# Two tiles transposed by the DMA engines instead of TensorE, and six units computed in halves of 256 columns

## The chip, the cores and the metric

The kernel runs on one core of a Trainium2 chip. Five engines work on it side by side, each with an instruction queue that is executed in order: TensorE (PE; its weight loads are shown apart as PEld), VectorE (DVE), ScalarE (ACT), GpSimd (POOL) and SyncE (SP). They wait for one another through semaphores. Transfers are done by 16 DMA engines; a transfer is issued by a queue, here SP's (q1 in the profile) or ScalarE's (q10). TensorE writes into PSUM, eight banks of 128 x 512 fp32 values. The metric is the device time of one execution in microseconds.

## The reference

`x` is 2048 tokens of 512 values in bf16. The output is `x` plus a linear attention with learnt softmax features plus a dense layer pair with Mish, both fed by the same layer norm:

```python
xn = _layernorm(x, axis=-1)                       # no scale, no shift, eps 1e-5
return x + _A_ref(xn, A_wqkv, A_w_phi, A_wo) + _B_ref(xn, B_w1, B_b1, B_w2)
# _A_ref: H = 32 heads of Dh = 16
pq = jnp.einsum("bhsd,hdf->bhsf", q, w_phi)       # the same for k
phi_q = jnp.concatenate([_softmax(pq, axis=-1), _softmax(-pq, axis=-1)], axis=-1)
kv = jnp.einsum("bhsf,bhsd->bhfd", phi_k, v)
z  = jnp.einsum("bhsf->bhf", phi_k)
num = jnp.einsum("bhqf,bhfd->bhqd", phi_q, kv)
den = jnp.einsum("bhqf,bhf->bhq", phi_q, z)[..., None] + 1e-6
o = num / den                                     # heads joined, then @ wo
# _B_ref: F = 1792
h = jnp.einsum("bsd,df->bsf", x, w1) + b1
act = h * jnp.tanh(sp)                            # sp = softplus(h)
return jnp.einsum("bsf,fd->bsd", act, w2)
```

## The kernel before

**Tiles and groups.** The tokens are 16 tiles of 128, in 4 groups of 4. `xnT` holds the normalised tokens transposed: for each tile four blocks of 128 channels by 128 tokens. It is needed by every projection: as the stationary operand for logits and values, as the moving operand for the first dense layer.

**The order by hand.** `STEPS` is one list of steps, executed from left to right when the program is built (lines 623 to 625). Every step appends its instructions to the queues of its engines. So the list fixes, for each engine, the order of its own work; between engines only data and buffers are waited for. `@n` names one of six PSUM banks (a shared buffer: a new owner waits until the old contents have been read); `a` and `v` say whether ScalarE or VectorE does the copy or inversion.

**The steps that matter here.**

- Opening, first group, tile by tile: `LS i` (statistics of tile i, VectorE), `RS i` (the inverse root, GpSimd), `AZ i` (normalise, VectorE), `TP i` (four TensorE transposes of 128 columns into a bank, line 560), `TC i` (copy into `xnT`, line 565).
- `F0 kt` (fold: key weights times the feature weights, four matmuls of 128 columns, line 156), `FD kt` (copy to `wkp`, line 165); `F`, `FC` the same for the queries. `WB` builds the block matrix for the folds, `KM` a mask, `PB` and `CB` turn and copy the bias.
- `LP`: the logits of tiles 0 and 1, eight matmuls of 512 columns (line 209), in pairs: both tiles with fold 0, then both with fold 1, and so on.
- `V t` (values of tile t, line 194) and `VC t` (copy, line 218); `L s i` (logits of stage s, tile i) and `LC s i` (copy, line 252); stages 0 to 3 are the keys of the groups, 4 to 7 the queries. `WL` is a logit step in the two banks beside the six.
- `H u` (unit u of the first dense layer: 128 of the 1792 hidden channels for one group of 512 tokens, four matmuls of 512 columns, line 228); u = 0 to 13 is group 0, 14 to 27 group 1. `M u` (Mish on ScalarE, line 239) frees its bank.
- `LN g`, `AP g k`: statistics of group g, and normalisation of its half k with a DMA transpose of two tiles issued by SP (line 186). `DX g` loads the tokens of group g (SP), `DW` loads the second layer's weights `w2` (2, three DMAs) and `wo` (3), `WT` the query weights.
- Softmax: `E s 0/1` (maxima and minima, VectorE, five operations each), `X` (exponentials, ScalarE), `S` (sums, VectorE), `R` (inversion), `N` (normalise), `A` (key-value matrices, TensorE); `KV`, `W`, `Q`, `G`, `C` for the queries; `C h` ends in a DMA transpose issued by SP.
- `O t` (second dense layer for tile t, 14 matmuls), `P t` (output projection), `Y t` (residual, and the store); `OH`, `PH`, `YH` the last tile in two parts.

ScalarE keeps one table set at a time: `M` needs one, `X`, `R a`, `W a` and `C a` another; the program loads a table when the set changes (line 138).

Before `STEPS` the loads are issued: on SP tile 0, the key weights transposed (`wT`), tiles 2 and 3, `wv`, half of `w1`, tiles 4 to 7, the other half of `w1`; on ScalarE the feature weights, tile 1 and the bias (lines 483 to 493). Twelve matmuls on constants run first (line 513).

Of the kernel before, what the change touches and what calls it, by code (L numbers as in the profile page):

```python
# [29 lines left out]
9; M 10; AP 1 1; H 11 @5; E 0 1; V 4 @1; X 0 1; WL 1; LN 2; V 6 @4; VC 4 a; X 0 0; L 1 0 @2; L 1 3  # L30
@0; LC 1 0 a; V 5 @3; LN 3; VC 5 a; H 12 @1; WL 2; H 13 @2; VC 6 a; S 0 0; LC 1 3 a; M 11; V 3 @3; M
12; M 13; H 14 @4; H 15 @0; H 16 @5; H 17 @1; VC 3 a; M 14; H 18 @2; M 15; M 16; M 17; LC 1 2 a; H
19 @3; AP 2 0; AP 2 1; AP 3 0; L 2 0 @4; LC 2 0 a; L 2 1 @0; LC 2 1 a; V 2 @5; S 0 1; L 2 2 @1; M
18; LC 1 1 a; M 19; H 20 @4; LC 2 2 a; AP 3 1; H 21 @0; WT; H 22 @2; M 20; VC 2 a; R 0 1 v; L 2 3
@3; H 23 @1; R 0 0 v; N 0 1; M 21; N 0 0; H 24 @4; M 22; LC 2 3 a; F 0 @5; F 1 @0; E 1 0; E 1 1; M
23; M 24; F 2 @2; E 2 0; E 2 1; FC 0 a; H 25 @3; H 26 @1; FC 1 a; H 27 @4; M 25; M 26; L 3 2 @5; FC
2 a; M 27; V 7 @0; L 3 3 @3; V 11 @1; F 3 @2; L 3 0 @4; LC 3 0 v; LC 3 2 a; L 3 1 @5; A 0 0; X 1 0;
X 1 1; A 0 1; LC 3 3 a; FC 3 v; S 1 0; V 8 @4; LC 3 1 a; VC 7 a; L 4 0 @2; E 3 0; VC 8 a; LC 4 0 a;
L 4 1 @3; LC 4 1 a; L 4 3 @5; VC 11 a; L 4 2 @0; X 2 0; V 9 @4; L 5 0 @2; H 28 @3; H 29 @1; VC 9 a;
LC 4 2 v; M 28; M 29; H 30 @0; H 31 @4; H 32 @3; M 30; H 33 @1; H 34 @0; M 31; M 32; M 33; M 34; H  # L40
35 @4; M 35; H 36 @3; M 36; S 1 1; LC 4 3 a; R 1 0 v; E 3 1; LC 5 0 a; N 1 0; R 1 1 v; H 37 @1; H 38
@0; H 39 @4; H 40 @3; H 41 @5; H 42 @2; S 2 0; A 1 0; M 37; N 1 1; M 38; M 39; M 40; A 1 1; M 41; M
42; X 3 0; L 6 3 @1; L 5 2 @0; V 10 @4; VC 10 a; L 5 1 @3; LC 5 2 a; L 6 0 @5; E 4 0; E 4 1; X 2 1;
S 3 0; V 15 @2; VC 15 a; V 13 @4; VC 13 a; LC 6 0 a; R 2 0 a; S 2 1; DW 3; R 3 0 a; X 3 1; L 6 1 @0;
LC 5 1 a; DW 2; N 3 0; N 2 0; L 5 3 @2; O 0 @4; S 3 1; V 12 @5; V 14 @3; LC 6 1 a; LC 5 3 a; O 1 @0;
L 6 2 @2; R 2 1 a; N 2 1; VC 14 a; LC 6 3 a; VC 12 v; R 3 1 a; N 3 1; X 4 0; A 2 0; S 4 0; LC 6 2 a;
A 2 1; A 3 0; W 4 0 v; X 4 1; H 43 @3; M 43; A 3 1; H 44 @1; H 45 @5; M 44; H 46 @2; M 45; H 47 @3;
M 46; M 47; H 48 @1; KV; H 49 @5; H 50 @2; Q 0 0; M 48; M 49; G 0 0; M 50; H 51 @3; H 52 @1; H 53
# [2 lines left out]
S 5 0; Q 1 0; L 7 3 @5; G 1 0; E 6 1; W 5 0 a; P 0; P 1; Y 0; Q 1 1; O 4 @1; G 1 1; LC 7 3 a; O 5
@4; S 5 1; Q 2 0; O 6 @5; C 1 a; P 2; G 2 0; W 5 1 v; Y 1; Q 2 1; P 3; O 7 @0; E 7 0; X 6 0; S 6 0;
G 2 1; Q 3 0; C 2 a; G 3 0; Y 2; Y 3; X 6 1; O 8 @2; Q 3 1; W 6 0 v; E 7 1; S 6 1; P 4; P 5; G 3 1;
C 3 a; Q 4 0; X 7 0; Y 4; W 6 1 v; X 7 1; S 7 0; O 9 @3; O 10 @1; G 4 0; Q 4 1; P 6; P 7; G 4 1; Y
# [601 lines left out]
```

## Time and profile before

| | us |
|---|---|
| three runs | 173.78, 173.98, 173.88; median 173.88 |
| the profiled execution | 174.0 |
| its span in the profile | 172.3 |
| TensorE busy | 168.7 (98%) |
| VectorE busy | 143.2 (83%) |
| ScalarE busy | 119.5 (69%) |

The span is what the profile covers, from the first to the last instruction; 1.7 us of the execution lie around it. Times in the text are microseconds from the span's start. A timeline line gives the start, the length, the engine, the line of the program, the operation, what it writes and reads, how many instructions it joins, and in brackets the idle time before them with what ended it. In a line on a stretch each engine has its busy time and, in parentheses, its instructions. A matmul's length contains its latency; the distance from one start to the next is what it costs in a row of them.

### The profile page before, as it was taken

The numbers are of one execution on the slowest core, as the hardware profiler recorded it, in microseconds if no ns is written. First come the engines' busy times: TensorE is split into PE (matmuls) and PEld (weight loads), VectorE is DVE, ScalarE is ACT, GpSimd is POOL, SyncE is SP. The second block draws the span as 40 slices with busy tenths as digits, with TensorE's granted clock in tenths as the row PEclk, the third lists the DMA queues.
The fourth block names the chain that finished last, engine by engine and source line by source line (L and its number), as shares of the span: only waits on it lengthen the run. The fifth ranks groups of instructions, "written<-read, shape, count | busy, mean of one in ns | idle before, by whom it ended". The sixth has DMA issues, their size and how long they took to land.

```text
span 172.3 us, 2713 instructions
## 1 busy us (share of the span) xinstructions
PE 168.7 (98%) x1039; PEld 82.4 (48%) x1039; DVE 143.2 (83%) x221; ACT 119.5 (69%) x192; POOL 9.4 (5%) x26
## 2 busy tenths in 40 slices
...
GB/s 98 269 377 365 82 98 0 37 189 207 366 120 0 0 4 0 0 0 0 4 0 0 64 118 66 12 51 67 150 152 93 150 95 144 172 168 100 173 134 61
DMA packets 44953, 18.02 MB, mean 105 GB/s; under 512 B 37004, under 2 KB 44940, under 8 KB 44940
## 3 DMA queue, kind: packets, MB, share of 16 engines
...
q10 hardware_dynamic: 844, 0.25, 0.6%
q8 instruction: 8, 0.13, 0.3%
...
## 4 chain that ended last, share of the span: by engine, by line
PE 95%; DMA 3%; SPq 0%; DVE 0%; issue 0%
PE po L463 28%; PE ph L228 28%; PE pl L194 14%; PE po L470 8%; PE pv L194 8%; DMA wT<-in_A_wqkv_dram 3%; PE pnd L418 2%; PE pkv L387 2%; PE pfold L156 1%; PE pwide L194 1%; PE pl L209 1%; PE ptr L560 0%; SPq L483 0%; DVE x_sb L477 0%; PE pb L533 0%
## 5 line engine op out<-in xcount | busy, mean ns | idle before, releaser
L463 PE MATMUL po<-w_sb,acts 128*128 128x512 bf16 (+2 forms) x238 | 50.7, 366 | 0.0
L228 PE MATMUL ph<-xnT,w_sb 128*128 128x512 bf16 x224 | 50.1, 379 | 0.0
L239 ACT ACTIVATE acts<-ph,b1f 128x512 bf16<-128x512 f32 x56 | 37.2, 694 | 4.6 <-PE ph L228 4.4
L305 DVE TENSOR_REDUCE s<-e 128x128 f32<-128x2048 bf16 x16 | 36.4, 2279 | 2.5 <-ACT e L288 2.5
L228 PEld LDWEIGHTS <-w_sb 128*128 128x128 bf16 x224 | 21.7, 98 | 25.5
L463 PEld LDWEIGHTS <-acts 128*128 128x128 bf16 x238 | 22.3, 98 | 24.1
L288 ACT ACTIVATE e<-e 128x2048 bf16<-128x2048 bf16 x16 | 30.3, 1908 | 0.0
L194 PEld LDWEIGHTS <-xnT 128*128 128x128 bf16 x184 | 17.6, 98 | 20.1 <-DMA wv<-in_A_wqkv_dram 0.2
L252 ACT CAST p_sb<-pl 128x512 bf16<-128x512 f32 x27 | 15.4, 587 | 5.5 <-PE pl L194 4.7
L433 ACT COPY ds<-pnd 128x32 f32<-128x32 f32 x16 | 2.9, 183 | 23.5 <-PE pnd L418 23.5
L194 PE MATMUL pv<-wv,xnT 128*128 128x512 bf16 x64 | 16.1, 379 | 0.0
L477 DVE TENSOR_TENSOR x_sb<-po,x_sb 128x512 bf16<-128x512 f32 (+2 forms) x17 | 10.9, 654 | 5.7 <-PE po L470 5.7
L470 PE MATMUL po<-wqk,xnT 128*128 128x512 bf16 (+2 forms) x68 | 15.5, 366 | 0.0
L194 PE MATMUL pl<-wqk,xnT 128*128 128x512 bf16 x64 | 15.3, 379 | 0.0
L170 DVE BATCH_NORM_STATS2 stats<-x_sb 128x6 f32<-128x512 bf16 x16 | 10.1, 679 | 4.3 <-DMA x_sb<-in_A_x_dram 4.3
L263 DVE TENSOR_TENSOR m<-m 128x512 bf16<-128x512 bf16 (+1 forms) x32 | 11.5, 358 | 1.1
L194 PE MATMUL pl<-wkp,xnT 128*128 128x512 bf16 x48 | 11.7, 379 | 0.0
L263 DVE TENSOR_TENSOR m<-p_sb 128x1024 bf16<-128x1024 bf16 x16 | 10.9, 682 | 0.2 <-ACT p_sb L252 0.2
L272 DVE TENSOR_TENSOR e<-p_sb,m 128x2048 bf16<-128x2048 bf16 x8 | 9.8, 1226 | 1.4 <-PE pkv L387 1.1
L272 DVE TENSOR_TENSOR e<-m,p_sb 128x2048 bf16<-128x2048 bf16 x8 | 9.8, 1225 | 0.3
L340 DVE TENSOR_TENSOR e<-e,r 128x2048 bf16<-128x2048 bf16 x8 | 9.6, 1215 | 0.0
L138 ACT ACT_TABLE_LOAD x7 | 9.0, 1283 | 0.1
...
## 6 DMA issues: line engine op xcount, KB each, us to landing
...
w_sb<-in_B_w_dram SPq DMA_DIRECT2D x2, 896.0 KB, 7.8
x_sb<-in_A_x_dram SPq DMA_DIRECT2D x3, 512.0 KB, 10.0
...
wv<-in_A_wqkv_dram SPq DMA_DIRECT2D x1, 512.0 KB, 4.5
wqk<-in_A_wo_dram SPq DMA_DIRECT2D x1, 512.0 KB, 4.6
w_sb<-in_B_w_dram SPq DMA_DIRECT2D x1, 512.0 KB, 9.6
...
```

What stands on the lines that cost most here:

```text
L170: nc.vector.bn_stats(stats[:, i, :], xs[:, i, :])
L194: nc.tensor.matmul(pp, lhsT=xnT[:, t, kt, :], rhs=w[:, kt, :], start=(kt == 0), stop=(kt == KT - 1),)
L228: nc.tensor.matmul(ph_of[u][:], lhsT=w1_sb[:, kt, f * P : (f + 1) * P], rhs=xnT[:, g * TPG : (g + 1) * TPG, kt, :], start=(kt == 0), stop= ...
L239: nc.scalar.activation(acts[:, f, g * 512 : (g + 1) * 512], ph_of.pop(u)[:], ACT.Mish, bias=b1f[:, f : f + 1])
L252: copy(p_of[s][:, i, :], pl_of.pop((s, i)))
L263: nc.vector.tensor_tensor(out=m[:], in0=src[:, :, 0:half], in1=src[:, :, half : 2 * half], op=op)
L272: nc.vector.tensor_tensor(out=e_of[s][:].rearrange("p t j l c -> p (t j) l c")[:, :, pl, :].rearrange("p t (c e o) -> p t c e o", e=8, o=2 ...
L288: nc.scalar.activation(v, v, ACT.Exp)
L305: nc.vector.reduce_sum(t[:], pair(s, k).rearrange("p t j l (c e) -> p (t j l c) e", e=16), axis=AX.X)
L463: nc.tensor.matmul(po_of[t, c.stop][:, c], lhsT=acts[:, f, t * P : (t + 1) * P], rhs=w2_sb[:, f, c], start=(f == 0), stop=False,)
L470: nc.tensor.matmul(po_of[t, c.stop][:, c], lhsT=oT_of[t // 2][:, t % 2 * 4 + j, :], rhs=wo_sb[:, j, c], start=False, stop=(j == 3),)
L477: nc.vector.tensor_tensor(out=y, in0=po_of.pop((t, c.stop))[:, c], in1=y, op=ALU.add)
```

## The change

- `TP 2`, `TP 3`, `TC 2` and `TC 3` go. In their place stand `AD 2` and `AD 3`: a DMA transpose of one tile each from the normalised tokens straight into `xnT`, issued from ScalarE's queue.
- The units 0 to 5 of the first dense layer are computed in two halves of 256 columns: `HA u b` for tiles 0 and 1, `HB u` for tiles 2 and 3, into the same bank; all six `HA` come first.
- Buffers: sums 6 instead of 3, the logarithm in place of its operand, `r2` 3 instead of 2, `r` 1 instead of 2.
- The order is written anew throughout: among others `TP 1` stands ahead of the folds, all four `FD` are ScalarE's, `DW 2` comes in the opening and `DX 3` later, `LN 2` ahead of `AP 1 0`, and other copies and inversions are ScalarE's or VectorE's than before.

```diff
--- before.py
+++ after.py
@@ -22,40 +22,40 @@
 WARM = 12
 STEPS = """
-LS 0; RS 0; DX 2; LS 1; WB; RS 1; AZ 0; TP 0 @0; F0 0 @1; F0 1 @2; AZ 1; FD 0 v; TP 1 @3; TC 1 v; LS
-2; PB @4; RS 2; TC 0 a; LS 3; RS 3; FD 1 a; AZ 2; F0 2 @5; F0 3 @0; FD 2 a; FD 3 a; LP i @1,2; KM;
-DX 3; AZ 3; V 0 @3; LC 0 0 a; TP 2 @5; V 1 @0; TC 2 a; TP 3 @1; VC 0 a; LC 0 1 v; TC 3 v; CB; L 0 2
-@5; L 0 3 @2; LC 0 3 a; LN 1; H 0 @3; H 1 @1; H 2 @4; M 0; LC 0 2 a; H 3 @2; M 1; M 2; M 3; VC 1 a;
...
-@5; S 4 1; W 4 1 v; M 51; M 52; H 54 @2; H 55 @3; Q 0 1; M 53; E 5 0; E 5 1; M 54; E 6 0; L 7 0 @1;
-M 55; G 0 1; C 0 a; X 5 0; LC 7 0 a; L 7 1 @5; X 5 1; O 2 @2; O 3 @3; LC 7 1 a; L 7 2 @1; LC 7 2 a;
...
-0; O 13 @0; Q 6 1; G 6 1; W 7 1 v; P 8; P 9; Q 7 0; C 6 a; G 7 0; P 10; P 11; Y 8; Q 7 1; G 7 1; O
-14 @2; Y 9; Y 10; C 7 a; P 12; P 13; OH 0 @3; PH 0; Y 11; P 14; OH 1 @1; PH 1; Y 12; Y 13; YH 0; Y
-14; YH 1
+KM; LS 0; LS 1; RS 0; WB; AZ 0; TP 0 @0; TC 0 a; DX 2; RS 1; AZ 1; TP 1 @1; F0 0 @2; F0 1 @3; TC 1
+v; FD 0 a; LS 2; FD 1 a; F0 2 @4; FD 2 a; LS 3; F0 3 @5; RS 2; AZ 2; FD 3 a; AD 2; RS 3; AZ 3; PB
+@0; AD 3; DW 2; LP i @1,2; V 1 @3; V 0 @4; VC 0 a; LC 0 0 v; LC 0 1 a; VC 1 v; HA 0 @5; HA 1 @1; HA
+2 @3; CB; HA 3 @0; HA 4 @4; HA 5 @2; LN 1; HB 0; HB 1; HB 2; M 0; LN 2; AP 1 0; HB 3; L 0 2 @5; HB
+4; M 1; M 2; M 3; M 4; HB 5; H 6 @1; M 5; M 6; L 0 3 @3; LC 0 3 a; AP 1 1; LC 0 2 a; H 7 @0; H 8 @4;
+M 7; H 9 @2; H 10 @1; M 8; DX 3; H 11 @3; M 9; M 10; H 12 @5; E 0 0; M 11; M 12; AP 2 0; H 13 @0; H
+14 @4; M 13; M 14; AP 2 1; WL 1; E 0 1; X 0 0; L 1 0 @2; V 3 @1; LN 3; VC 3 a; LC 1 0 a; L 2 1 @3; L
+2 0 @5; S 0 0; L 2 2 @0; AP 3 0; L 2 3 @4; H 15 @1; H 16 @2; LC 2 0 a; LC 2 1 a; H 17 @5; LC 2 2 a;
+X 0 1; R 0 0 a; M 15; M 16; AP 3 1; WT; WL 2; LC 2 3 v; M 17; H 18 @3; H 19 @0; M 18; LC 1 1 v; E 2
+0; M 19; E 2 1; L 1 3 @4; H 20 @1; H 21 @2; H 22 @5; LC 1 2 a; M 20; LC 1 3 a; M 21; M 22; H 23 @3;
+V 6 @0; E 1 0; S 0 1; M 23; H 24 @1; M 24; H 25 @4; M 25; VC 6 a; H 26 @2; F 0 @5; M 26; F 1 @3; FC
+1 a; H 27 @1; H 28 @4; M 27; H 29 @0; H 30 @2; M 28; M 29; H 31 @3; E 1 1; M 30; M 31; H 32 @1; M
+32; F 2 @4; X 1 0; V 2 @0; V 8 @2; V 4 @3; FC 2 a; FC 0 v; V 9 @5; L 3 1 @1; VC 4 a; R 0 1 v; VC 2
+v; F 3 @0; FC 3 a; N 0 0; A 0 0; VC 8 a; X 1 1; L 3 0 @4; N 0 1; VC 9 v; L 3 2 @3; S 1 0; S 1 1; L 4
+3 @0; L 3 3 @2; LC 3 0 a; LC 3 3 a; LC 3 1 a; L 4 0 @5; V 7 @4; LC 3 2 a; R 1 0 a; R 1 1 a; LC 4 0
+a; X 2 1; VC 7 v; L 4 1 @2; LC 4 1 v; LC 4 3 v; V 5 @1; VC 5 a; L 4 2 @3; V 12 @4; N 1 0; X 2 0; H
+33 @2; A 0 1; H 34 @5; H 35 @0; LC 4 2 v; N 1 1; M 33; M 34; E 3 0; H 36 @3; A 1 0; H 37 @1; A 1 1;
+S 2 1; M 35; E 4 0; H 38 @2; VC 12 a; V 11 @5; M 36; H 39 @0; H 40 @4; M 37; M 38; VC 11 a; M 39; E
+3 1; M 40; H 41 @3; H 42 @1; H 43 @2; H 44 @5; H 45 @0; L 6 0 @4; M 41; M 42; S 2 0; DW 3; L 5 0 @3;
...
+M 51; KV; Q 0 0; G 0 0; W 4 1 v; M 52; H 53 @5; H 54 @3; E 5 0; L 7 2 @0; M 53; M 54; E 5 1; Q 0 1;
+G 0 1; L 7 0 @1; C 0 a; LC 7 0 a; LC 7 2 a; O 2 @5; L 7 1 @3; X 5 0; Q 1 0; O 3 @1; G 1 0; Q 1 1; G
+1 1; E 6 0; S 5 0; P 0; P 1; Y 0; C 1 a; Y 1; H 55 @0; W 5 0 v; LC 7 1 a; L 7 3 @4; X 5 1; S 5 1; O
+4 @3; O 5 @2; M 55; LC 7 3 a; E 6 1; Q 2 0; W 5 1 a; G 2 0; E 7 0; P 2; Y 2; O 6 @0; Q 2 1; X 6 0; P
...
+P 9; C 5 a; W 7 1 a; G 6 0; Y 7; Q 6 1; G 6 1; O 13 @4; Q 7 0; Y 8; Y 9; P 10; P 11; G 7 0; Q 7 1; O
+14 @5; OH 0 @1; C 6 a; G 7 1; C 7 v; P 12; P 13; P 14; Y 10; Y 11; PH 0; OH 1 @3; PH 1; Y 12; Y 13;
+Y 14; YH 0; YH 1
@@ -233,6 +233,19 @@
                 stop=(kt == KT - 1),
             )
 
+    def hidden_half(u, i, b=None):
+
+        if i == 0:
+            ph_of[u] = bank(b, "ph")
+        for kt in range(KT):
+            nc.tensor.matmul(
+                ph_of[u][:, i * 256 : (i + 1) * 256],
+                lhsT=w1_sb[:, kt, u * P : (u + 1) * P],
+                rhs=xnT[:, 2 * i : 2 * i + 2, kt, :],
+                start=(kt == 0),
+                stop=(kt == KT - 1),
+            )
+
     def mish(u):
         g, f = divmod(u, FT)
         table("mish")
@@ -301,7 +314,7 @@
 
     def sums(s, k):
 
-        t = s_of[s, k] = smx.tile([P, 128], FP32, name="s", bufs=3)
+        t = s_of[s, k] = smx.tile([P, 128], FP32, name="s", bufs=6)
         nc.vector.reduce_sum(
             t[:], pair(s, k).rearrange("p t j l (c e) -> p (t j l c) e", e=16), axis=AX.X
         )
@@ -315,21 +328,20 @@
             out, src.rearrange("p (c o) -> p c o", o=1).to_broadcast([P, n, 2]), ACT.Exp, scale=scale
         )
 
-    def log(src, n):
+    def log(v):
 
         table("natural_log_exp_and_others")
-        t = smx.tile([P, 128], FP32, name="log")
-        nc.scalar.activation(t[:, 0:n], src, ACT.Ln)
-        return t[:, 0:n]
+        nc.scalar.activation(v, v, ACT.Ln)
+        return v
 
     def invert(s, k, how):
 
         t = s_of.pop((s, k))
-        r2 = r_of[s, k] = smx.tile([P, 128, 2], BF16, name="r2")
+        r2 = r_of[s, k] = smx.tile([P, 128, 2], BF16, name="r2", bufs=3)
         if how == "a":
-            power(r2[:], log(t[:], 128), 128, -1.0)
+            power(r2[:], log(t[:]), 128, -1.0)
             return
-        r = smx.tile([P, 128], BF16, name="r")
+        r = smx.tile([P, 128], BF16, name="r", bufs=1)
         with nc.allow_low_precision("the softmaxes are bf16"):
             nc.vector.reciprocal(r[:], t[:])
         nc.vector.tensor_copy(r2[:], r[:].rearrange("p (c o) -> p c o", o=1).to_broadcast([P, 128, 2]))
@@ -348,7 +360,7 @@
         q = smx.tile([P, 16, 4], FP32, name="q")
         r2 = smx.tile([P, 16, 4, 2], BF16, name="q2")
         if how == "a":
-            t4 = log(t[:], 128).rearrange("p (t l c) -> p t l c", l=2, c=4)
+            t4 = log(t[:]).rearrange("p (t l c) -> p t l c", l=2, c=4)
             nc.vector.tensor_tensor(
                 out=q[:], in0=t4[:, :, 0, :], in1=t4[:, :, 1, :], op=ALU.subtract
             )
@@ -444,7 +456,7 @@
         f = opool.tile([P, 64, 2], BF16, name="f")
         d = ds[:].rearrange("p i j c -> p (i j c)")
         if how == "a":
-            power(f[:], log(d, 64), 64, -1.0)
+            power(f[:], log(d), 64, -1.0)
         else:
             w = opool.tile([P, 64], FP32, name="w")
             nc.vector.reciprocal(w[:], d)
@@ -564,6 +576,9 @@
     def first_keep(i, copy):
         copy(xnT[:, i, :, :], pf_of.pop(("t", i))[:].rearrange("p (k c) -> p k c", k=KT))
 
+    def first_turn_dma(i):
+        nc.scalar.dma_start_transpose(out=xnT[:, i, :, :], in_=xn_of[0][:, i, :])
+
     def stats(g):
         ln_of[g] = moments_of()
         st, mv, rstd = ln_of[g]
@@ -609,7 +624,8 @@
         "LN": stats, "AP": apply, "DX": load_tokens, "DW": load_weights, "WL": wide,
         "L": logits, "LC": lambda s, i, c: take(s, i, copies[c]),
         "V": value, "VC": lambda t, c: keep(t, copies[c]),
-        "H": hidden, "M": mish,
+        "H": hidden, "M": mish, "AD": first_turn_dma,
+        "HA": lambda u, b: hidden_half(u, 0, b), "HB": lambda u: hidden_half(u, 1),
         "E": extremes, "X": exponentials, "S": sums,
         "R": invert, "N": normalise, "A": accumulate,
         "KV": mask_kv, "W": weigh, "Q": attend, "G": gather, "C": combine,
```

More of the change, by code (lines that the diff above doesn't have):

```diff
@@ L24 @@
 STEPS = """
-LS 0; RS 0; DX 2; LS 1; WB; RS 1; AZ 0; TP 0 @0; F0 0 @1; F0 1 @2; AZ 1; FD 0 v; TP 1 @3; TC 1 v; LS
-2; PB @4; RS 2; TC 0 a; LS 3; RS 3; FD 1 a; AZ 2; F0 2 @5; F0 3 @0; FD 2 a; FD 3 a; LP i @1,2; KM;
-DX 3; AZ 3; V 0 @3; LC 0 0 a; TP 2 @5; V 1 @0; TC 2 a; TP 3 @1; VC 0 a; LC 0 1 v; TC 3 v; CB; L 0 2
-@5; L 0 3 @2; LC 0 3 a; LN 1; H 0 @3; H 1 @1; H 2 @4; M 0; LC 0 2 a; H 3 @2; M 1; M 2; M 3; VC 1 a;
-E 0 0; H 4 @3; H 5 @5; AP 1 0; H 6 @1; H 7 @4; M 4; H 8 @2; M 5; H 9 @0; M 6; M 7; H 10 @3; M 8; M
@@ L30 @@
[L30 to L48, printed above, removed]
-@5; S 4 1; W 4 1 v; M 51; M 52; H 54 @2; H 55 @3; Q 0 1; M 53; E 5 0; E 5 1; M 54; E 6 0; L 7 0 @1;
@@ L50 @@
-M 55; G 0 1; C 0 a; X 5 0; LC 7 0 a; L 7 1 @5; X 5 1; O 2 @2; O 3 @3; LC 7 1 a; L 7 2 @1; LC 7 2 a;
[L51 to L54, printed above, removed]
@@ L55 @@
-5; Y 6; C 4 a; Q 5 0; W 7 0 a; G 5 0; O 11 @4; Q 5 1; Y 7; O 12 @5; S 7 1; G 5 1; C 5 a; Q 6 0; G 6
-0; O 13 @0; Q 6 1; G 6 1; W 7 1 v; P 8; P 9; Q 7 0; C 6 a; G 7 0; P 10; P 11; Y 8; Q 7 1; G 7 1; O
-14 @2; Y 9; Y 10; C 7 a; P 12; P 13; OH 0 @3; PH 0; Y 11; P 14; OH 1 @1; PH 1; Y 12; Y 13; YH 0; Y
-14; YH 1
+KM; LS 0; LS 1; RS 0; WB; AZ 0; TP 0 @0; TC 0 a; DX 2; RS 1; AZ 1; TP 1 @1; F0 0 @2; F0 1 @3; TC 1
+v; FD 0 a; LS 2; FD 1 a; F0 2 @4; FD 2 a; LS 3; F0 3 @5; RS 2; AZ 2; FD 3 a; AD 2; RS 3; AZ 3; PB
```

8 lines of the change are left out of this document (added).

## The prediction

> **What bounds the kernel now.** I read the page's busy shares and its chain first, then the chain in order of time, the opening in order of time, the stretches by engine, and last the DMA issues with their landings.
>
> ```profile
> span 172.3 us, 2713 instructions
> ...
> PE 168.7 (98%) x1039; PEld 82.4 (48%) x1039; DVE 143.2 (83%) x221; ACT 119.5 (69%) x192; POOL 9.4 (5%) x26
> ...
> PE 95%; DMA 3%; SPq 0%; DVE 0%; issue 0%
> ```
>
> The chain that ends last is TensorE for 95% of the span. In order of time it reads (start, length, what):
>
> ```profile
> 6.65 0.62 PE pfold L156 x8
> 7.27 0.22 PE ptr L560 x4
> ...
> 8.16 1.73 PE pl L209 x8
> 9.88 0.86 PE pv L194 x4
> ...
> 13.78 10.36 PE ph L228 x48
> ...
> 169.41 0.24 PE po L470 x4
> ```
>
> From 6.65 to 169.65 every piece begins where the one before it ends. The stretch from 6.65 to 169.65 has 162.99 us of PE busy in 163.00. So TensorE waits for nothing after its first weights. A new order can only take TensorE work away or add waits. It can't remove a wait, since there is none. A 512-column matmul costs 10.36/48 = 0.2158 us and a 128-column transpose 0.22/4 = 0.0555 us.
>
> The opening and the normalisation of the second group of tokens (start, length, engine, line, operation):
>
> ```profile
> 6.45 0.41 DVE L181 TENSOR_SCALAR xn<-x_sb,mv,rstd 128x512 bf16<-128x512 bf16 x1 [0.48 <-POOL rstd L177]
> 7.08 0.69 DVE L165 CAST wkp<-pfold 128x512 bf16<-128x512 f32 x1 [0.22 <-PE pfold L156]
> 7.31 1.74 ACT L165 CAST wkp<-pfold 128x512 bf16<-128x512 f32 x3
> 8.00 1.89 PE L209 MATMUL pl<-wkp,xnT 128*128 128x512 bf16 x8
> 13.43 2.47 DVE L170 BATCH_NORM_STATS2 stats<-x_sb 128x6 f32<-128x512 bf16 x4 [0.83 <-DMA x_sb<-in_A_x_dram]
> 15.82 0.36 DVE L172 BATCH_NORM_AGGREGATE mv<-stats 128x2 f32<-128x6 f32 x4
> 19.04 1.38 DVE L181 TENSOR_SCALAR xn<-x_sb,mv,rstd 128x512 bf16<-128x512 bf16 x4
> ```
>
> The folded weights are copied by two engines side by side, VectorE one and ScalarE three, so that the first logits run without a break. Four tiles' statistics take VectorE 13.43 to 16.18, 2.75 us.
>
> Loads fill the DMA engines in that time, and the transposes come after them (stretch, its length, busy time of each engine, clock, DMA share, GB/s):
>
> ```profile
> 9.70:13.60 3.90, 3.90 (x25) 2.01 (x24) 2.25 (x8) 1.66 (x3) 0.97 (x3) 1.00 1.06 373
> 13.60:17.40 3.80, 3.80 (x19) 1.76 (x18) 3.73 (x11) 3.12 (x6) 1.05 (x2) 1.00 1.08 361
> 17.40:18.80 1.40, 1.40 (x8) 0.59 (x6) 1.33 (x3) 1.40 (x3) 0.72 (x1) 1.00 0.43 130
> 18.80:25.00 6.20, 6.20 (x30) 2.84 (x29) 6.06 (x13) 5.30 (x8) 0.00 (x0) 1.00 0.45 86
> ```
>
> The DMA issues that matter, asked for one at a time (size, us from issue to landing): the first half of w1 is issued at 5.54 and lands at 11.9; tokens 8 to 11 are issued at 7.36 and land at 17.36; the second transpose of the second group is issued at 21.15.
>
> ```profile
> w_sb<-in_B_w_dram SPq DMA_DIRECT2D x1, 896.0 KB, 6.4
> x_sb<-in_A_x_dram SPq DMA_DIRECT2D x1, 512.0 KB, 10.0
> xnT<-xn SPq DMA_TRANSPOSE x1, 3.4
> ```
>
> **The change, part by part.** The sum is made against the profiled execution, 174.0 us (span 172.3, 1.7 around it); the runs' median is 173.88, 0.07% below.
>
> *TensorE's own work.* TP 2 and TP 3 go: 8 x 0.0555 = -0.44 us, straight off the path. Their copies (0.59 on ScalarE, 0.42 on VectorE) go too; neither was on the path. The halves: from 128 to 512 columns a matmul grows by (215.8-55.5)/384 = 0.417 ns a column, so 256 columns cost 109 ns and two halves 218, 2.2 ns more than one whole; 24 pairs: +0.05. Together -0.39.
>
> *The opening.* Now TP 1 stands ahead of the folds on TensorE and waits for AZ 1, which ends at 6.86 (6.45 + 0.41) as before: VectorE and GpSimd come to it in the same order. TP 1 runs 6.91 to 7.15, the folds F0 0 to F0 3 follow at 0.22 us each, and the first is through at 7.53 (a matmul's own 0.22 latency counted) where it was at 7.05. All four copies FD are ScalarE's now, 0.58 each: 7.57 to 9.90, against 9.05. The first logits need the fourth copy for their last pair: 9.95 + 2 x 0.216 = 10.38. Before, the values began at 9.72. So TensorE is 10.38 - 9.72 = 0.66 us later with the same work done. What covered this were the folds ahead of TP 1 and VectorE's share of the copies; both covers are gone. Bounds: 0 if the copies did not hold the logits, 0.85 if TC 0 or a slow hand-over delays the first copy by 0.2.
>
> *The third and fourth tile.* KM moves to VectorE's front, where it idles until 3.18, and LC 0 0 and VC 1, now VectorE's, end near 12.5, before tokens 4 to 7 land at 13.4: nothing. AZ 2 and AZ 3 end near 10.1 and 10.96 (before: 10.33 and 11.20, each now 0.24 earlier because TC 1 no longer stands behind a fold's copy). ScalarE issues the two transposes behind FD 3, at 10.15 and 11.0; an issue on SP takes 1.25 us for twice the size, so 0.63 each. Behind them wait VC 0 and LC 0 1, whose banks TensorE wants at 13.9 and 14.3; they end near 12.9 and 13.5, so the issues cost nothing, and up to 1.25 each would still be covered. TensorE: values to 12.11 (w1's first half lands 11.9), six HA of 0.437 to 14.73, then HB 0 needs both tiles. Their landing: 2.6 to 3.4 us after 11.0 by the transpose row, 13.6 to 14.4, in time; the row had idle DMA engines, so the upper end is a rival below.
>
> *The second group's tokens.* The first step that needs them all is now H 14, at 14.73 + 6 x 0.437 + 2 x 0.863 + 8 x 0.863 = 25.99; it needs AP 1 1 landed, and all of TensorE's queue stands behind it. LN 2 now stands ahead of AP 1 0 on VectorE, so AP 1 waits for tokens 8 to 11. Those land at 17.36, later by what the two new transposes take from full DMA engines: two transposes of twice the size took 0.45 x 6.20 = 2.79 us of the engines, so these two 1.39. With a share of 1.06 there is hardly room; I take 1.2 (bounds 0 and 1.39): 18.56. LN 2 ends 21.33, AP 1 0 is issued 0.76 later as before (19.04 to 19.80), 22.09, AP 1 1 1.35 behind it, 23.44, landing 3.4 later: 26.84. TensorE waits 0.85. Bounds: 0 (landing at 25.64), and 1.4: w2's 1792 KB, now issued ahead of it on SP, need 5 us at 361 GB/s and hold the queue until 23.5, 0.4 longer than AP 1 0's first packets like. Its three issues (2.1 us on SP) and DX 3 behind AP 1 1 delay no one else: SP idles until 22, and LN 3 comes after E 0 1.
>
> *The rest of the order.* Gains: none possible. VectorE had E 0 0 between LN 1 and AP 1; now it idles from 16.2 to 18.6. From 30 to 62 us it is busy 29.98 of 32 and ScalarE 29.79, so they have little to give. I walked the banks after H 14 with the rows' durations: H 20 waits 0.1 for M 15, H 27 0.15 for M 24, L 3 0 0.25 for FC 2 (it stands behind X 1 0 and its 1.28 table load), V 7 0.05 for LC 3 0: +0.55, bounds 0 and 1.5. Three inversions leave VectorE (1.24 each) for ScalarE (0.73); eleven copies of logits and values are VectorE's (0.69) where four were: with the copies it loses in the opening (0.69 and 0.42), nothing net. Table loads by the order: nine instead of seven, both new ones around M 55; from H 55's end ScalarE needs 4.5 us there and TensorE has 7 us of L 7 3, O 4 and O 5 to do. The tail has the same steps; C 7 on VectorE is covered by O 14, OH 0, P 12 and P 13 (7.0 us). The buffers (sums, r2, logarithm in place) take no wait off TensorE, which had none: 0.
>
> Sum: 174.0 - 0.39 + 0.66 + 0.85 + 0.55 = 175.67, called **175.7**.
>
> **The rivals.**
>
> *Nothing waits after the opening.* The DMA engines take the new transposes beside the loads, tokens 8 to 11 land by 17.7, AP 1 1 by 25.99, and banks have slack. 174.0 - 0.39 + 0.66 = 174.27. For it: the 0.85 hangs on one landing, which I can place only between bounds 1.4 apart. Against: engine shares of 1.06 and 1.08. It decides where tokens 8 to 11 land less than 0.35 us later than before.
>
> *The opening isn't later.* If the copies don't hold the logits and nothing else waits, only the work is left: 173.61, faster by 0.22%. Against it: the order of waits AZ 1, fold, copy, logits is fixed on three engines.
>
> *The two transposes starve.* ScalarE's queue shares full engines with SP's. The loads move 23 B/ns an engine, 77 ns for a 1792 B piece; a transpose moves 11.7 B/ns, 22 ns for its 256 B. Each engine has 64 such pieces; if they alternate one for one with w1's, they take 64 x 99 ns = 6.3 us and land near 17.8 instead of 14.4. HB 0 then waits 3 us, which swallows the 0.85: 174.27 + 3.0 + 0.2 = 177.5. In the one stretch where both queues worked, 2.1 to 2.9 us, it was otherwise:
>
> ```profile
> q10 hardware_dynamic: 600, 0.09, 64.6%
> q1 hardware_dynamic: 98, 0.08, 34.3%
> ```
>
> Six packets of ScalarE's queue went for each of SP's. [...]
>
> *VectorE becomes the bound in the middle.* Summed in program order with the rows' durations, VectorE has 58.2 us to do by TensorE's 60th microsecond of work, 55.9 before, and it idles 2.4 us more in the opening. 4.7 us more against 2.3 of slack and TensorE's delay of 1.1 leaves 1.3 late, and ScalarE has 1.4 more; if TensorE waits for both in full, 175.1 + 2.4 = 177.5. Against: most of it is softmax that is used much later.
>
> **How the numbers follow.** Forecast 0.55 (own range 174.8 to 176.6), nothing waits 0.13, starving 0.14, VectorE 0.13, opening free 0.05. A change under 0.2% (0.35 us) can't be told from none. Faster 0.05; same 0.13, the 174.27 of the first rival; slower 0.82. The range runs from 174.2, with the first rival, to 177.6, with the two slow ones' middles; outside are the fast case and their upper halves, under 0.2.
>
> **What would show it.** Right: PE pieces with gaps near 8 to 10 us; the value matmuls from 10.4; HB 0 with no wait; a wait of xnT's DMA ahead of H 14 near 26 us; VectorE's LN 2 released by x_sb's DMA near 18.5. Wrong: PE dense from 10.4 on (the first rival), LDWEIGHTS or matmuls of the second halves released by a DMA at 17 (starving), or PE waiting for DVE between 45 and 90.

## The result and the profile after

The changed kernel takes 181.34 us (median of 4 runs, 181.02 to 182.46); beside it the kernel before takes 173.84 (4 runs, 173.78 to 173.98). The ratio is 1.0442, with a 95% interval of 1.0396 to 1.0488: slower by 7.5 us. The forecast was 175.7, its range 174.2 to 177.6: the direction was right, the size was not. The profiled execution of after is the slowest of its four, 182.46 us with a span of 180.7, 8.4 us longer than the span of before. By their mean granted clocks, two of the four executions (182.46 and 181.50, at 0.981) spent some 6.8 us at half clock and the other two (181.19 and 181.02, at 0.990) some 3.4; what follows is the slowest one, told in full.

The page of after (span; PE's row of part 1; the granted clock in 40 slices; the chain's shares):

```profile
span 180.7 us, 2747 instructions
...
PE 171.0 (95%) x1055; PEld 85.3 (47%) x1055; DVE 143.3 (79%) x221; ACT 120.6 (67%) x193; POOL 8.9 (5%) x26
...
PEclk9999569999999999999999999999999999999999
...
PE 88%; DMA 6%; DVE 2%; POOL 1%; issue 0%; ACTq 0%
```

TensorE has 0.4 us less work by its own rows, and still shows 2.3 us more busy time: part of it ran at half clock, in the fifth and sixth slice. In the chain DMA has 6% where it had 3%.

TensorE's waits in after (line, what was waited for: us in total, times, longest). Before, the line of `warm` was the only one:

```profile
PE ph L241 <- DMA xnT<-xn: 4.1, 1, 4.1
PE ph L241 <- DMA w_sb<-in_B_w_dram: 1.0, 1, 1.0
PE ptr L572 <- DVE xn L181: 0.9, 2, 0.5
PE warm L525 <- PEq L656: 0.8, 1, 0.8
```

The first wait is HB 0's, for the transposes of tiles 2 and 3; the second is HA 0's, for w1's first half. Where they stand, in the timeline of after (start, length, engine, line, operation, and in brackets the idle time before and its releaser):

```profile
10.15 2.70 ACTq L580 DMA_TRANSPOSE xnT<-xn  x2
10.22 1.89 PE L194 MATMUL pv<-wv,xnT 128*128 128x512 bf16 x8
13.14 2.79 PE L241 MATMUL ph<-xnT,w_sb 128*128 128x256 bf16 x24 [1.03 <-DMA w_sb<-in_B_w_dram]
14.59 2.47 DVE L170 BATCH_NORM_STATS2 stats<-x_sb 128x6 f32<-128x512 bf16 x4 [2.32 <-DMA x_sb<-in_A_x_dram]
19.68 2.47 DVE L170 BATCH_NORM_STATS2 stats<-x_sb 128x6 f32<-128x512 bf16 x4 [2.34 <-DMA x_sb<-in_A_x_dram]
20.04 3.60 PE L241 MATMUL ph<-xnT,w_sb 128*128 128x256 bf16 x16 [4.11 <-DMA xnT<-xn]
```

The two issues start at 10.15, as forecast, but take 2.70 us together; the six HA units run 13.14 to 15.93, and HB 0 starts at 20.04. The statistics rows give the landings of tokens 4 to 7 (14.6; before 13.4) and 8 to 11 (19.65; before 17.36). The chain of after has the whole wait as one piece of DMA:

```profile
11.57 8.43 DMA xnT<-xn
20.00 0.05 issue
20.04 3.60 PE ph L241 x16
```

What the engines carried in that time, by queue, from 12 to 18 us (q1 is SP's queue, q10 ScalarE's; packets, MB, share of the 16 engines), with one issue's landing:

```profile
q1 hardware_dynamic: 1396, 1.78, 93.4%
q10 hardware_dynamic: 745, 0.18, 17.2%
...
xnT<-xn ACTq DMA_TRANSPOSE x1, 8.4
```

Packet by packet, the first 256 B piece of ScalarE's queue moves at 14.3, 4.2 us after the first issue; until then SP's queue alone moves. From 14.3 to 19.2 the two queues move nearly the same number of pieces: in each half microsecond from 15.5 to 19.0, 87 to 143 pieces of 256 B go, beside 100 to 143 of SP's, most of them 1024 B, four times the size.

The stretches by engine (stretch, length, busy time of PE, PEld, DVE, ACT, POOL, then granted clock, DMA share, GB/s):

```profile
15.80:20.04 4.24, 0.13 (x2) 0.00 (x0) 1.90 (x8) 0.00 (x0) 1.28 (x2) 0.85 1.14 306
20.04:25.60 5.56, 5.56 (x23) 3.34 (x24) 3.65 (x12) 2.75 (x4) 1.35 (x2) 0.50 0.97 255
25.60:32.00 6.40, 6.40 (x34) 3.23 (x33) 2.58 (x5) 5.36 (x9) 0.00 (x0) 1.00 0.53 133
...
92.00:177.90 85.90, 85.90 (x580) 43.21 (x578) 70.81 (x95) 52.33 (x96) 0.00 (x0) 1.00 0.50 96
```

The clock falls to 0.5 at 18.79, in the wait, and stays there for 6.83 us, to 25.62: 5.56 us of TensorE's work run at half speed. Behind that the profile shows no idle time of PE up to its last matmul.

So the 8.4 us of span can be laid out along TensorE, by how much the starts of its matmuls stand apart beyond their own length: own work -0.39; opening +0.39, and first turn 0.11 later; w1's first half +1.19; HB 0's wait +4.33; half clock +2.70. Sum 8.33, by which TensorE's last matmul ends later than before.

### The profile page after: what moved, and what is told of

It reads as the page before. It is cut to its first block, busy times and chain, and to the rows that moved or that the text cites. A ratio compares the mean times of both kernels' runs of the same rounds, so it can differ in the third digit from the quotient of the medians.

```text
span 180.7 us, 2747 instructions
## 1 busy us (share of the span) xinstructions
PE 171.0 (95%) x1055; PEld 85.3 (47%) x1055; DVE 143.3 (79%) x221; ACT 120.6 (67%) x193; POOL 8.9 (5%) x26
## 4 chain that ended last, share of the span: by engine, by line
PE 88%; DMA 6%; DVE 2%; POOL 1%; issue 0%; ACTq 0%
PE po L475 27%; PE ph L228 24%; PE pl L194 14%; PE po L482 8%; PE pv L194 7%; DMA xnT<-xn 5%; PE ph L241 3%; PE pnd L430 2%; PE pkv L399 2%; DMA x_sb<-in_A_x_dram 2%; POOL rstd L177 1%; PE pwide L194 1%; DVE stats L170 1%; PE pfold L156 0%; DVE xn L181 0%; POOL rstd L176 0%
## 5 line engine op out<-in xcount | busy, mean ns | idle before, releaser
L228 PE MATMUL ph<-xnT,w_sb 128*128 128x512 bf16 x200 | 45.8, 379 | 0.0
L228 PEld LDWEIGHTS <-w_sb 128*128 128x128 bf16 x200 | 19.1, 98 | 21.8
L194 PE MATMUL pl<-wqk,xnT 128*128 128x512 bf16 x64 | 15.9, 379 | 0.0
L194 PE MATMUL pv<-wv,xnT 128*128 128x512 bf16 x64 | 15.6, 379 | 0.0
L265 ACT CAST p_sb<-pl 128x512 bf16<-128x512 f32 x24 | 13.2, 589 | 0.8 <-PE pl L194 0.8
L194 PE MATMUL pl<-wkp,xnT 128*128 128x512 bf16 x48 | 12.6, 400 | 0.0
L241 PE MATMUL ph<-xnT,w_sb 128*128 128x256 bf16 x48 | 7.7, 328 | 5.1 <-DMA xnT<-xn 4.1
```

The costliest lines, as they stand in the source:

```text
L194: nc.tensor.matmul(pp, lhsT=xnT[:, t, kt, :], rhs=w[:, kt, :], start=(kt == 0), stop=(kt == KT - 1),)
L228: nc.tensor.matmul(ph_of[u][:], lhsT=w1_sb[:, kt, f * P : (f + 1) * P], rhs=xnT[:, g * TPG : (g + 1) * TPG, kt, :], start=(kt == 0), stop= ...
L241: nc.tensor.matmul(ph_of[u][:, i * 256 : (i + 1) * 256], lhsT=w1_sb[:, kt, u * P : (u + 1) * P], rhs=xnT[:, 2 * i : 2 * i + 2, kt, :], sta ...
L265: copy(p_of[s][:, i, :], pl_of.pop((s, i)))
```

## The experiments

The theory at the start: the two transposes, put into a second queue beside full DMA engines, land 5 us too late, HB 0 holds all of TensorE, and the wait takes the clock down with it. Rivals: w2's loads, issued earlier now, are what they share with; ScalarE's queue is slow by itself; the new order loses on its own and only shows here. A diff below is of the order's steps, compared step by step, and of code; `...` stands for what is left out.

**Without w2 (e1).** After, with w2's load moved back to where before had it, behind DW 3.

```
-AD 3; DW 2; LP i @1,2
+AD 3; LP i @1,2
-DW 3; L 5 0 @3
+DW 3; DW 2; L 5 0 @3
```

> The changed kernel with the three loads of w2 back beside wo (DW 2 behind DW 3), out of the opening. Sharing (the two transposes of ScalarE's queue are slow because SP's loads are in flight): w1's second half and tokens 8 to 11 are still there until about 18, so the second transpose lands at 17 to 19.5 instead of 20.0, HB 0 waits 1.5 to 3.5 us instead of 4.3, total 177 to 180.5. Rival w2 (the three loads of w2 alone hold them): it lands near 14.5, no wait, total 175.5 or less. Rival queue (a transpose from ScalarE's queue takes 8 us by itself): 20.0 as before, total 181.

180.32 us (179.58 to 181.24), ratio 1.0375 (1.033 to 1.0421). TensorE's waits:

```profile
PE ph L241 <- DMA xnT<-xn: 3.5, 1, 3.5
PE warm L525 <- PEq L656: 0.8, 1, 0.8
PE ph L241 <- DMA w_sb<-in_B_w_dram: 0.6, 1, 0.6
```

About one of the 7.5 us goes; the wait is still 3.5 and the first piece of ScalarE's queue still comes 4.3 us after its issue. w2 is not the main cause: w1's second half and tokens 8 to 11, which before had in flight as well, are enough.

**Tiles 2 and 3 on TensorE again (e2).** The rest of the change stays: order, halves, opening, buffers, w2 early; the bias's copy (`CB`) goes in between.

```
-AD 2
-AD 3
 V 1 @3
+TP 2 @5; TC 2 a
 V 0 @4
+CB; TP 3 @0; TC 3 a
 ...
-CB
```

> The changed kernel with tiles 2 and 3 turned by TensorE again (TP 2 and TP 3 with ScalarE's copies between and behind the values; CB earlier), everything else as in the changed kernel. All theories that put the loss on the two DMA transposes: no wait at HA 0 or HB 0, no drop of the clock, and what is left is the opening's order and the halves, 0.4 + 0.05 us above the kernel before: 174.3 to 174.8. Rival (the new order costs by itself, in waits for banks or VectorE): over 176.

174.41 us (173.98 to 174.9), ratio 1.0022 (1.001 to 1.0033). Its waits are those of before:

```profile
core 0 of [0], span 172.3 us
engine line waited for: us in total, times, longest us
PE warm L525 <- PEq L656: 0.8, 1, 0.8
```

6.9 of the 7.5 us hang on these two transposes (the profiled execution, 174.0, is one of the two fastest of ten). The rest of the new order, the halves and the opening cost 0.47 us together.

**Loads held back (e4).** The transposes stay on ScalarE's queue; SP waits until they have landed (`HO`, a copy of 4 KB that reads tile 3's transpose) and only then issues tokens 8 to 11, w1's second half (`W1`, its load moved into the order) and w2.

```
-DX 2; RS 1
+RS 1
-AD 3; DW 2
+AD 3; HO; DX 2; W1; DW 2
+def hold():
+    held = consts.tile([P, 16], BF16, name="held")
+    nc.sync.dma_start(held[:], xnT[:, 3, 0, 0:16])
 ...
-nc.sync.dma_start(w1_sb[:, :, 7 * P : F], w1_v[:, :, 7 * P : F])
+def second_half():
+    nc.sync.dma_start(w1_sb[:, :, 7 * P : F], w1_v[:, :, 7 * P : F])
```

> The changed kernel with the loads behind tokens 4 to 7 held back: SP waits in a small transfer that reads the tile of AD 3, and then issues tokens 8 to 11, w1's second half and w2. The transposes stay on ScalarE's queue. Sharing: they meet only the ends of w1's first half and of tokens 4 to 7, AD 3 lands at 14 to 16, HB 0 waits 0 to 1 us; tokens 8 to 11 land near 17.5 to 18.5, H 14 waits 0 to 2 us; total 174.5 to 177.5. Rival queue: AD 3 lands near 20 again, the loads behind it later still, total over 182.

180.15 us (179.62 to 181.56), ratio 1.0366 (1.0321 to 1.0411), where 174.5 to 177.5 was expected. The issues with their landings (operation, size, median us to landing), of 8 to 30 us:

```profile
w_sb<-in_B_w_dram SPq DMA_DIRECT2D x1, 896.0 KB, 7.9
...
xnT<-xn ACTq DMA_TRANSPOSE x2, 3.5
```

and in the timeline:

```profile
12.10 4.54 PE L241 MATMUL ph<-xnT,w_sb 128*128 128x256 bf16 x40
23.62 8.85 PE L228 MATMUL ph<-xnT,w_sb 128*128 128x512 bf16 x32 [3.52 <-DMA w_sb<-in_B_w_dram]
```

With only the end of tokens 4 to 7 beside them (SP's last pieces of them go before 13), the same two transposes land 3.5 us after issue in the median, at 14.0 and 14.5 where the forecast had 13.6 to 14.4, and HA and HB run through without a break. Their first piece moves 2.2 us after the issue, and all of them within 1.7 us, where after took 4.9. So ScalarE's queue isn't slow by itself; it is the sharing with SP's loads. The time isn't won, since w1's second half is now the late one: a wait of 3.52, and the clock at half for 3.4 us behind it. It took 7.9 us for 896 KB, with half as many pieces in a half microsecond (41 to 62) as the same loads had in after (about 100); why, these runs don't show.

**The transposes on SP, in front of the loads (e6).** `W1` is the same as in e4.

```
-nc.scalar.dma_start_transpose(out=xnT[:, i, :, :], in_=xn_of[0][:, i, :])
+nc.sync.dma_start_transpose(out=xnT[:, i, :, :], in_=xn_of[0][:, i, :])
-DX 2; RS 1
+RS 1
-AD 3; DW 2
+AD 3; DX 2; W1; DW 2
```

> The changed kernel with the two transposes issued from SP's queue ahead of the loads that used to be in front of them: SP issues tokens 4 to 7, AD 2, AD 3, tokens 8 to 11, w1's second half, w2. Nothing of ScalarE's queue. Theory sharing and order: the transposes' pieces follow tokens 4 to 7, land at 13.5 to 14.8, no wait at HB 0, none at H 7 (w1's second half lands near 18.5), a wait of 0 to 1 us at H 14; total 174.0 to 175.3, and no drop of the clock. Rival (a transpose of a tile in this stretch is slow wherever it is issued): a wait at HB 0 of over 2 us, total over 177.

176.39 us, ratio 1.0143 (1.0126 to 1.0161), where 174.0 to 175.3 was expected. Four of the five executions take 176.25 to 176.47; the fifth takes 179.18, at a mean clock of 0.988. HB 0 waits no more (landings 13.3 and 13.8). The wait has moved to H 14, for the second group's transposes, and is 2.36 us where 0 to 1 was expected. Its timeline:

```profile
13.41 2.57 SPq L606 DMA_DIRECT2D w_sb<-in_B_w_dram  x3
19.59 5.32 SPq L186 DMA_TRANSPOSE xnT<-xn  x2
27.84 1.02 PE L228 MATMUL ph<-xnT,w_sb 128*128 128x512 bf16 x4 [2.36 <-DMA xnT<-xn]
```

The two issues of AP 1 take 5.32 us behind w2's load, which lands at 21.7 to 25.1, and AP 1 1 lands at 27.7.

**The same with w2 late (e9).** If w2 holds AP 1 up, this wait must go with w2.

```
-W1; DW 2; LP i @1,2
+W1; LP i @1,2
-DW 3; L 5 0 @3
+DW 3; DW 2; L 5 0 @3
```

> As the kernel with the transposes on SP in front of the loads (176.39), but with w2's three loads back beside wo. Theory (its wait of 2.5 us ahead of H 14 is the second group's transpose standing in SP's queue behind w2): the transpose lands at 24.0 to 24.8, H 14 at 25.1 doesn't wait, total 173.7 to 174.2. Rival (the transpose is late because tokens 8 to 11 are): a wait of 1 us or more remains, 175 and over.

174.28 us (173.83 to 174.8), ratio 1.002 (1.001 to 1.003). The two issues take 2.62, AP 1 1 lands at 24.19, and H 14, which TensorE reaches at 26.15, doesn't wait:

```profile
12.27 4.54 PE L241 MATMUL ph<-xnT,w_sb 128*128 128x256 bf16 x40 [0.41 <-DMA w_sb<-in_B_w_dram]
19.73 2.62 SPq L186 DMA_TRANSPOSE xnT<-xn  x2
20.11 7.07 PE L228 MATMUL ph<-xnT,w_sb 128*128 128x512 bf16 x32
```

From 12.3 us to its last matmul TensorE has no idle time in this execution. The new order thus has no bank wait of its own.

**The wait filled with matmuls (e3).** After, with 20 matmuls of constants into a spare bank ahead of HB 0, so that TensorE isn't idle for long.

```
-LN 1; HB 0
+LN 1; FI 20; HB 0
```

> The changed kernel with 20 matmuls of 512 columns on constants ahead of HB 0, 4.3 us at the full clock, into the two banks beside the six; their result is used nowhere. Theory clock (the half clock from 18.8 to 25.6 us comes from the idle wait of 4.3 us and costs 2.7 us): the transposes land at 20.0 as before, the clock stays 1.00, total 178.5 to 179. Rival (the clock falls for another reason, or the fillers only push the work): 181.3 or more.

181.05 us (179.57 to 181.75), ratio 1.0394 (1.0343 to 1.0445). The clock stays at 1.00 to the tail, as expected, yet the time hardly moves: in the profiled execution tile 3 lands at 21.14, 1.1 later than in after, and TensorE still waits behind the matmuls:

```profile
14.60 4.54 PE L533 MATMUL fill<-const-bfloat16-1.0 128*128 128x512 bf16 x20
21.18 1.92 PE L241 MATMUL ph<-xnT,w_sb 128*128 128x256 bf16 x16 [2.05 <-DMA xnT<-xn]
```

Near the end it also waits 0.7 us for qT's DMA. A miss, and inconclusive: the landing moved along with what was tested. The next pair has no DMA transpose at that place.

**An idle wait with no transfer in it, and the same filled (e11, e12).** Both are e2 (tiles on TensorE), with HB 0 waiting for GpSimd: eight memsets of a buffer that is written over later, then an addition of 0 to four columns of tile 3. e12 has 22 constant matmuls ahead of HB 0 as well.

```
 TC 3 a
+PW 8
-LN 1; HB 0
+LN 1; FI 22; HB 0          (e12 alone)
+for _ in range(8):
+    nc.gpsimd.memset(acts[:, 13, 512:2048], 0.0)
+nc.gpsimd.tensor_scalar(out=xnT[:, 3, 0, 0:4], in0=xnT[:, 3, 0, 0:4], scalar1=0.0, scalar2=None, op0=ALU.add)
```

> The kernel with the turns of tiles 2 and 3 on TensorE (174.41), in which HB 0 is made to wait some 4 to 5 us for GpSimd, which clears a stretch of acts that is written later eight times and then adds 0 to four columns of tile 3. No transfer is changed. Theory clock: the granted clock falls to 0.5 some 3 us into the wait and stays there for 3.4 or 6.8 us; total 174.4 + the wait (4 to 5) + 1.7 to 3.4. Rival (no fall without the transfers): 174.4 + the wait alone.

> The same wait for GpSimd, filled with 22 matmuls of 512 columns on constants (4.75 us). Theory clock: the clock stays 1.00 and the total is 1.7 to 3.4 us below the unfilled one, 174.4 + the wait. Rival (filling doesn't help, as the kernel with fillers beside the transposes might be read: 181.05 against 181.34): the same total as unfilled.

184.19 us (183.76 to 185.11) idle, 181.57 (181.27 to 181.71) filled: 2.6 us less with 22 matmuls more. The idle wait of e11 came out at 6.96 us where 4 to 5 had been expected. The timeline of e11, with the stretch from 22 to 24 us (as above; the granted clock stands third from the end), and then the same of e12:

```profile
21.80 3.40 PE L241 MATMUL ph<-xnT,w_sb 128*128 128x256 bf16 x16 [6.96 <-POOL xnT L541]
...
22.00:24.00 2.00, 2.00 (x11) 1.44 (x10) 0.89 (x3) 0.99 (x2) 1.89 (x3) 0.50 0.03 9
```

```profile
15.00 4.98 PE L533 MATMUL fill<-const-bfloat16-1.0 128*128 128x512 bf16 x22
22.12 1.91 PE L241 MATMUL ph<-xnT,w_sb 128*128 128x256 bf16 x16 [2.15 <-POOL xnT L541]
...
22.00:24.00 2.00, 1.88 (x17) 1.66 (x17) 0.56 (x2) 1.24 (x3) 1.83 (x5) 1.00 0.06 20
```

HB 0 starts equally late in both, 16.07 and 16.06 us after the first turn; the same 16 matmuls take 3.40 in the one and 1.91 in the other. In e11 the clock is 0.5 from 18.05 to 24.88, in e12 it is 1.00 up to the tail. So a wait costs more than itself: in this pair 1.5 us of slow matmuls in the profiled executions (and a later wait of 0.8 for qT's DMA, which e12 doesn't show), 2.6 us in the medians.

**Before's opening, with the transposes on SP (e7) and on TensorE (e8).** The first two folds stand ahead of TP 1 again, and VectorE copies the first; on e6 and on e2.

```
 TC 0 a
+F0 0 @2; F0 1 @3
 RS 1; AZ 1
+FD 0 v
 TP 1 @1
-F0 0 @2; F0 1 @3
 TC 1 v
-FD 0 a
```

> As the kernel with the transposes on SP in front of the loads, and with the opening of the kernel before: the folds 0 and 1 ahead of TP 1, the first copy (FD 0) on VectorE. The step of 0.31 to 0.39 us that the new opening costs should go: values from 9.7 to 9.8, total lower by 0.3 to 0.4 than without it, 173.6 to 175. If nothing waits, only the two turns less on TensorE are left: 173.5, below the kernel before. Rival (AZ 2 and AZ 3 come 0.24 later on VectorE and the transposes with them): the gain is eaten by a wait at HB 0.

> As the kernel with the turns of tiles 2 and 3 on TensorE (174.41), with the opening of the kernel before (folds 0 and 1 ahead of TP 1, FD 0 on VectorE). If the opening's order is what is left of its loss, 0.3 to 0.4 us go: 174.0 to 174.1. Rival (the rest is somewhere else): 174.4 still.

e7: 178.93 us (176.75 to 179.29), ratio 1.0257 (1.0214 to 1.0301), slower than e6 by 2.5 where it should have been faster. H 14's wait is the same as in e6; here the clock falls after it (timeline of e7):

```profile
28.80 1.82 PE L228 MATMUL ph<-xnT,w_sb 128*128 128x512 bf16 x4 [2.42 <-DMA xnT<-xn]
30.42 1.91 PE L194 MATMUL pwide<-wkp,xnT 128*128 128x512 bf16 x4
```

The clock is 0.5 from 28.88 to 32.30. Of six executions four have a mean clock of 0.99 and take 178.9 to 179.3 us, two have 1.00 and take 176.75 and 177.19: the fallen clock goes with some 2 us (in e6's fifth execution with 2.8), and whether it falls after a wait of 2.4 isn't settled by the kernel. So the 2.5 us between the medians of e6 and e7 is in the main how many of the executions met it, not what the opening costs. Every half-clock stretch between the opening and the tail of a profiled execution here lasts some 3.4 us (e1, e4, e7) or 6.83 (after, e11).

In the 3.4 us before the clock fell TensorE had worked 0.2 us in e11, 0.5 in after, 1.0 in e7, 1.1 in e4 and 1.3 in e1. The waits that the falls go with are, in the same order, 6.96, 4.11, 2.42, 3.52 and 3.53 us. Waits of 2.36 (e6), 2.15 (e12) and 2.05 (e3) left the clock at 1.00 in their profiled executions. What tells e6's 2.36 from e7's 2.42, these runs don't show.

e8: 174.21 us (173.8 to 175.42), ratio 1.0023 (1.0006 to 1.004), where 174.0 to 174.1 was expected: not to be told from e2's 174.41. In its profile the opening is as before (values 3.70 us after the first turn; before 3.69), and the next load takes it back:

```profile
PE ph L241 <- DMA w_sb<-in_B_w_dram: 0.5, 1, 0.5
```

**The halves alone (e5).** Before, with its first six units as HA u; HB u, one behind the other.

```
-H 0 @3; H 1 @1; H 2 @4
+HA 0 @3; HB 0; HA 1 @1; HB 1; HA 2 @4; HB 2
 ...
```

> The kernel before with the units 0 to 5 in two halves of 256 columns each (HA u and HB u in the place of H u), nothing else changed. By the rows a half costs 109 ns a matmul: 24 pairs x 2.2 ns = 0.05 us, total 173.9 to 174.0, not to be told from the kernel before. Rival (a second weight load for each pair can't be hidden behind 256 columns): 24 x 98 ns more at most, up to 176.

174.07 us (173.85 to 174.25), ratio 1.0011 (1.0003 to 1.002): 0.18 us, between 0.05 and 0.35. The estimate of 0.05 is the lower end; by the lengths of its matmuls the trace has 0.06, and the second weight loads are hidden.

**All mended at once (e10).** e9 with before's opening, and w1's first load cut in two (units 0 to 2, units 3 to 6) so that HA 0 needn't wait for all of it; the opening's steps are changed as in e7.

```
-nc.sync.dma_start(w1_sb[:, :, 0 : 7 * P], w1_v[:, :, 0 : 7 * P])
+nc.sync.dma_start(w1_sb[:, :, 0 : 3 * P], w1_v[:, :, 0 : 3 * P])
+nc.sync.dma_start(w1_sb[:, :, 3 * P : 7 * P], w1_v[:, :, 3 * P : 7 * P])
```

> As the one before, and with the opening of the kernel before (folds 0 and 1 ahead of TP 1, FD 0 on VectorE) and w1's first load cut in two (units 0 to 2, units 3 to 6), so that HA 0 doesn't wait for it. If neither w1 nor a transpose is waited for, TensorE's work is 0.39 us less than in the kernel before and nothing else differs on the path: 173.5 to 173.6, below it by 0.2%. Rival (the third and fourth tile come 0.24 us later, or w1 does): 173.9 to 175.

174.79 us (174.08 to 175.21), ratio 1.0048 (1.0031 to 1.0066): a miss; it should have beaten before by 0.3. Both mends did what they should: the w1 wait is gone, and HA 0 starts at 11.52. What they laid bare is the transposes again (timeline of e10):

```profile
11.52 2.88 PE L241 MATMUL ph<-xnT,w_sb 128*128 128x256 bf16 x24
14.78 1.92 PE L241 MATMUL ph<-xnT,w_sb 128*128 128x256 bf16 x16 [0.38 <-DMA xnT<-xn]
```

Tile 3 lands at 14.74 here and at 14.64 in e9; there w1's lateness had covered it. In this execution (174.57) the waits give +0.74 and the turns' work -0.39 back, 0.35, against 0.6 by the spans. That the median stands 0.9 above before is not explained in full.

## Why the prediction was right or wrong

**What bounds the kernel: right.** TensorE had no wait to lose, so the change could only take work away or add waits; every microsecond lost is a wait of TensorE or a slower clock of it.

**TensorE's own work, -0.39: right.** It is the whole possible gain of the DMA turns, and e2, which gives 0.44 of it back, is 6.9 us faster.

**The opening, +0.66: right in mechanism, too large.** The values begin at 10.22, 4.08 us after the first turn, against 3.69 before: 0.39, and the waits of `ptr` for xn are where the text put them. In e2 the same opening shows 3.75 in its profile, so its cost varies with when VectorE's second tile is ready (0.50 us after the first turn in e2, 0.83 in after). That it holds TensorE shows little in the time (e2 against e8); in e8's profile w1's first half stands right behind it.

**The third and fourth tile, 0: the step that failed.** It had three numbers. The issues' start, 10.15, was right. "0.63 each" was wrong: one tile's issue takes 1.28 to 1.32 us, as long as two tiles' on SP (1.23 to 1.29 in before), so here it didn't go by size; that cost nothing, as its bound said. "Landing 13.6 to 14.4, in time" was wrong by 5.6 us: it took the landing from a row with idle engines, and gave the row's other condition to a rival. With the engines' share of 1.06 in plain view, the cover (HB 0 only at 14.73) should have been charged with the sharing. e4 shows the row to be right where the loads are held back, 3.5 us in the median. The 20.0 costs 4.33 us of wait and 2.70 of half clock, 7.0 of the 8.3, on a step that the sum had at 0.

**The rival "the two transposes starve", 177.5: the mechanism that happened.** Equal numbers of pieces are what the trace shows, and the moving itself took 4.9 us against 6.3 worked out. The rival was too cheap by two terms: the moving began 4.2 us after the first issue, so that the landing was at 20.0 instead of 17.8; and nothing was charged for the clock. The 0.2 in its sum has no row behind it, and no run shows it. Corrected: 174.27 + 4.33 (HB 0) + 2.70 (clock) = 181.30; with w1's 1.19 and an opening smaller by 0.27 that is 182.22, 0.24 below the profiled execution's 182.46. The text held the six-to-one count of 2.1 to 2.9 us against it. The rival's own assumption, one piece for one, was the better guide: in after, 100 to 143 pieces of the one queue and 87 to 143 of the other go in each half microsecond from 15.5 to 19.0 us; in what turns they go, such counts don't show. In the stretch from 2.1 to 2.9 SP's queue had only the rest of tile 0's 128 pieces of 1024 B to give, and most of ScalarE's 600 were of 32 B, so the count told little of a queue that is full.

**w1's first half, "lands 11.9": wrong by 1.2.** It lands at 13.09, 0.57 after the second-slowest of its 16 engines, and HA 0, which comes 0.44 earlier without the turns, waits 1.19. In the next three loads of that execution too the last engine is 0.57 to 0.82 behind; in before's profile it is 0.18 to 0.19, in e2's 0.13 to 0.14. So the lag differs from execution to execution, and comes ahead of the transposes' first piece. The margin of 0.2 us in the text was no margin; e1, e7, e8 and e9 wait 0.4 to 0.6 at the same place, e2 not at all.

**The second group's tokens, +0.85: not seen in after; its lower bound, 0, is what came.** Tokens 8 to 11 land at 19.65 where 18.56 was estimated, but TensorE is by then 7 us late itself, and H 14 waits for nothing. With TensorE on time (e2) AP 1 1 lands at 25.16 and there is no wait either: tokens 8 to 11 land at 16.84 there, with no transposes beside them. w2 holding the queue, which the text had as its upper bound, is real: 2.36 us in e6, none in e9.

**The rest of the order, +0.55: wrong.** In these profiles it is 0: from H 6 on, after, e9 and e10 are dense to TensorE's last matmul, e9 and e10 with TensorE nearly on time. (In e3 and e11 TensorE waits 0.7 and 0.8 us near the end for qT's DMA, so the tail isn't free of waits in every execution.) The lags that the walk over the banks gave ScalarE and VectorE don't show. The rival of VectorE in the middle falls with them: it never becomes the bound. Without the transposes' wait the change comes out where the rival "nothing waits" had it, at 174.27: e2 at 174.41, e9 at 174.28. That they agree to so little is in part luck: e2 has the two turns' 0.44 back on TensorE, and e9's sum is made of another opening (0.39) and a wait for w1 (0.41) that the rival doesn't have.

**The sum.** Of the terms, -0.39 + 0.66 stood as causes, 0.85 and 0.55 were not there, and 4.33 + 2.70 + 1.19 were missing: the first two come from one landing estimated in one place, the third from w1's landing.
